# First matrix product of a convolution + MLP kernel issued as 64-row halves, with its weights doubled on both partition halves and partly streamed

## The chip, the cores and the metric

The kernel runs on one core of a Trainium2 chip. A core has a matrix engine (PE, with weight loads listed apart as PEld), a vector engine (DVE), a scalar engine (ACT), a general engine (POOL) and a small engine that here only issues DMAs (SP). The metric is the device time of one execution in microseconds (us). Times in the profile views are in us from the start of the span, unless marked ns.

## The reference

```python
# x (8, 4096, 192), weight (8, 7), w_in (192, 2048), w_out (2048, 192)
w = softmax(weight, axis=-1)                      # 8 heads, 7 taps
x_pad = concatenate([zeros(B, 6, D), x], axis=1)
a[b, s, h*24:(h+1)*24] = sum_k w[h, k] * x_pad[b, s + k, h*24:(h+1)*24]
h = a.reshape(32768, 192) @ w_in
out = (h * sigmoid(1.702 * h)) @ w_out
```

A causal convolution over seven positions with one set of taps per head, then two matrix products with a sigmoid-weighted activation between them. The weights of the products arrive as 64-bit floats.

## The kernel before

**Tiling.** The 32768 tokens are cut into 32 stretches, called bigs, of 1024 tokens: two sequences (n = 0, 1) of 512 tokens, each cut again into two halves of 256 (o = 0, 1). The 2048 hidden features are cut into 16 units of 128. For every big the kernel runs `hidden` (the first product, 16 units) and then `second` (the second product, whose order is written out by hand in `PLAN`, a fast-multiplication scheme of 25 products on sums of blocks of `g` and sums of blocks of `w_out`). Big 0 has its own code (`first_step`, `second_plain`), since the weights are converted from their 64-bit words while it runs.

**The first product.** The operands are split in two parts each, and three products are added up: `upper_high` (weights `wh`, tokens `xh`), `upper_low` (`wl`, `xl`) and `lower` (a ring slot, `xd`). Each of the three is one call of `pass_of`, and there are 48 passes per big. The 192 input features are a block of 128 and a block of 64. A pass is two matmuls over 128 rows (L215, one for each token half o) and two over 64 rows (L221); of the latter, o = 0 lies on partitions 0 to 63 and o = 1 on 64 to 127, and they start together. `phase` turns the order around from pass to pass, so that the 64-row matmuls of two neighbouring passes stand side by side, and the 128-row ones too. All matmuls have 512 columns of tokens and write one PSUM bank each; a unit owns a slot of two banks, and four slots rotate.

**Order in `hidden`.** For unit i the PE order is `upper_high(i)`, `lower(i-2)`, `upper_low(i)`. After `upper_low(i)` the two banks are multiplied by a constant (`scale`, L237, on ACT or DVE as `SCALES` says: "av" is one half on each, "vv" both on DVE). `lower(i)` needs that scale; `gelu` (L241, two ACT instructions) follows it, and `upper_high(i+4)` needs the gelu, as it writes the same slot. `lower(15)` (`end_unit` of the last unit) is issued as `end`, a little into `second`. The call `extra(i)` at the end of unit i puts other work in line: the input of the big after next (`load_x`, SP, at unit 0), the last three convolution taps and their sums (`next_tap`, L500 on ACT at units 0, 2 and 3; `add_taps`, L517, mostly on POOL), three 32x32 transposes of the input on DVE (`transpose_x`, L161, units 7, 8, 9), and the first ten sums of blocks of `g` (`EARLY_G`, L607, units 10 to 15: nine on DVE, one as an accumulating DMA from POOL). The sum of `EARLY_G` listed as number 6 (unit 13) reads what that DMA wrote.

**Weights.** `wh` and `wl` stay in SBUF for all 16 units. The third part is streamed from DRAM through `ring`, six slots of 128 x 256; after `lower` of ring entry q, `load_ring(q + 6)` is issued on SP.

**Queues.** SP issues all input loads, ring loads and output stores in program order; each may wait for a semaphore, and what stands behind it waits too. ACT, DVE and POOL also work strictly in order.

**The start.** In `first_step`, weight piece j (of 8, two units each) goes through `split` (DVE, ACT), `round_w_in` (three DVE instructions, then ACT L437 writes `wh`, POOL L438, ACT `wl`, POOL L440 the ring slot, and SP stores it). This is issued in `extra(i)` for even i, for piece i/2 + 1.

Of the kernel before, what the change touches and what calls it, by code (L numbers as in the profile page):

```python
# [16 lines left out]
def kernel(  # L17
# [27 lines left out]
    NJ2 = TOK // Q + 1  # L45
    n3 = NC * Q
    assert B % 2 == 0 and NC == 3 and D == NC * R and HD == 3 * Q and S % TOK == 0
    assert D == P + R and PAD <= Q
# [65 lines left out]

    turned = [consts.tile([P, 2, n * Q], F32, name=f"xt{i}") for i, n in enumerate((NJ2, NJ))]
    own = consts.tile([P, 6, T], F32)
    flat_own = own.rearrange("p b t -> p (b t)")
    xh, xl, xd = (consts.tile([P, 6, T], F32R, name=f"x{i}") for i in "hld")
    NX1, NX2 = 2 * NJ2 * Q, 2 * NJ * Q

    def xin_of(big):
        flat = flat_room if big == 2 else flat_g(NG - 1)
        return (
            flat[:, 0:NX1].rearrange("p (n j d) -> p n j d", n=2, j=NJ2),
            flat[:, NX1 : NX1 + NX2].rearrange("p (n j d) -> p n j d", n=2, j=NJ),
        )

    def load_x(big, parts=(0, 2, 1)):

        p, c = divmod(big, CHUNKS)  # L130
        one, two = xin_of(big)
        fill = nc.gpsimd if big else vec

        def load(dst, n, t, d, j):
            nc.sync.dma_start(  # L135
                out=dst[:, j:, :],
                in_=x_v[n, p, t + j * Q : t + dst.shape[1] * Q, d : d + Q].rearrange("(j i) d -> i j d", i=Q),
            )

        for a in parts:  # L140
            if a < 2:
                if c == 0:
                    fill.memset(one[:, a, 0, :], 0.0)
                for q in range(4):
                    load(one[q * Q : (q + 1) * Q, a], a, c * TOK - Q, q * Q, int(c == 0))
            else:
                if c == 0:
                    fill.memset(two[0:R, :, 0, :], 0.0)
                for n in range(2):
                    for q in range(4):  # L150
                        o, v = divmod(q, 2)
                        load(
                            two[q * Q : (q + 1) * Q, n], n, c * TOK + o * T - Q, P + v * Q, int(c == 0 and o == 0)
                        )

    def transpose_x(big, a):
        xin = xin_of(big)
        src, dst = (xin[0][:, a], turned[0][:, a]) if a < 2 else (xin[1], turned[1])
        if a == 2:
            src, dst = src.rearrange("p n j d -> p (n j) d"), dst.rearrange("p n t -> p (n t)")  # L160
        vec.transpose(dst.rearrange("p (j t) -> p j t", t=Q), src)  # L161

    def conv_src(a, k):
        at = slice(Q - PAD + k, Q - PAD + k + (TOK if a < 2 else T))
        return turned[0][:, a, at].rearrange("p (o t) -> p o t", o=2) if a < 2 else turned[1][:, :, at]

    def tap_of(a, k):
        return cw[:, a // 2, k : k + 1]

    def own_of(a):  # L170
        return own[:, 2 * a : 2 * a + 2, :]

    def conv(a, k, times=vec.tensor_scalar_mul):
        src, dst, tap = conv_src(a, k), own_of(a), tap_of(a, k)
        if k == 0:
            times(dst, src, tap)
        else:
            vec.scalar_tensor_tensor(  # L178
                out=dst, in0=src, scalar=tap, in1=dst, op0=ALU.mult, op1=ALU.add
            )  # L180
# [18 lines left out]
    wd_dram = dram.tile([N_W, P, 2, 2 * P], F32)  # L199

    def load_ring(q):
        if q < NF * N_BIG:
            r = q % NF
            nc.sync.dma_start(
                out=wide(ring[:, q % RING]).rearrange("p k f -> p (k f)"), in_=wd_dram[r // 2, :, r % 2, :]
            )

    phase = [0]

    def pass_of(slot, w, t, first=False, last=False):  # L210
        phase[0] += 1
        for step in range(2):
            if (step + phase[0]) % 2:
                for o in range(2):
                    nc.tensor.matmul(  # L215
                        slot[o], w[:, 0, :], t[:, o : o + 3 : 2, :],
                        start=first and step == 0, stop=last and step == 1, skip_group_check=True,
                    )
            else:
                for o in range(2):  # L220
                    nc.tensor.matmul(  # L221
                        slot[o], w[halves[o], 1, :], t[halves[o], 4:6, :],
                        start=first and step == 0, stop=last and step == 1, skip_group_check=True,
                    )
# [4 lines left out]
    def upper_low(slot, r):  # L229
        pass_of(slot, wl[:, r], xl)  # L230

    def lower(slot, q):
        pass_of(slot, ring[:, q % RING], xd, last=True)
# [13 lines left out]
    def end_unit(big, tiles, r):  # L247
        q = big * NF + r
        lower(tiles[r % 4], q)
        gelu(tiles[r % 4], r)  # L250
        if q + RING >= NF:
            load_ring(q + RING)

    def hidden(big, tiles, scales, extra, begun=True):

        for i in range(NF):
            if i or not begun:
                upper_high(tiles[i % 4], i)
            if i > 1:
                end_unit(big, tiles, i - 2)  # L260
            if i or not begun:
                upper_low(tiles[i % 4], i)
            scale(tiles[i % 4], scales[i])
            extra(i)
# [50 lines left out]
    PART = 4 * P  # L315
    PIECE = CW * D
    raw = [flat_g(2)[:, 2 * PART * i : 2 * PART * (i + 1)] for i in range(4)]
    free = flat_g(3)[:, NX1 + NX2 :]
    raw += [free[:, 2 * PART * i : 2 * PART * (i + 1)] for i in range(2)]
    raw += [osbs[:, 0 : 2 * PART], flat_own[:, 0 : 2 * PART]]  # L320
    raw_out = [flat_room[:, 2 * PIECE * i : 2 * PIECE * (i + 1)] for i in range(3)] + [osbs[:, 0 : 2 * PIECE]]
    assert 2 * PART <= 4 * T and NX1 + NX2 + 4 * PART <= 4 * BLK and 6 * PIECE <= 5 * BLK
    words_in = [flat_form[:, 2 * PART * i : 2 * PART * (i + 1)] for i in range(3)]
    words_out = [flat_form[:, 6 * PART + 2 * PIECE * i : 6 * PART + 2 * PIECE * (i + 1)] for i in range(2)]
    assert 6 * PART + 4 * PIECE <= FORMS * NG * HD
    diag = flat_room[:, 4 * PIECE : 4 * PIECE + K * P].rearrange("p (k q) -> p k q", k=K)
    all_sel = osbs[:, 2 * PIECE : 2 * PIECE + 2 * P].rearrange("i (c q) -> i c q", c=2)
    sel = all_sel[0:H]
    ident = osbs[:, 2 * PIECE + 2 * P : 2 * PIECE + 3 * P]
    assert 2 * PIECE + 3 * P <= 4 * TOK  # L330
# [10 lines left out]
    load_x(0, (0, 2))  # L341

    w_in_v = moe_w_in.bitcast(U32)
    w_out_v = moe_w_out.bitcast(U32).rearrange("(c p) d -> p c d", p=P)

    def load_w_in(j):
        dst = raw[j].bitcast(U32).rearrange("p (r k f) -> p r k f", r=2, k=2)
        cols = slice(4 * P * j, 4 * P * (j + 1))
        for on, k, rows in ((slice(0, P), 0, 0), (halves[0], 1, P), (halves[1], 1, P)):
            n = on.stop - on.start  # L350
            nc.sync.dma_start(
                out=dst[on, :, k, :], in_=w_in_v[rows : rows + n, cols].rearrange("q (r f) -> q r f", r=2)
# [9 lines left out]
    load_x(0, (1,))  # L362
# [4 lines left out]
    for c in range(2):  # L367
        part = sel[:, c, :].rearrange("i (h q) -> i h q", h=2)
        for sign in (1, -1):
# [5 lines left out]
                base=P * c if sign == 1 else group - 1 - P * c,  # L375
                pattern=[[0 if c else sign * R, 2], [sign, R]],
# [14 lines left out]
    def in_part(j):  # L391
        return raw[j], words_in[j % 3]
# [35 lines left out]
    def round_w_in(j):  # L428
# [3 lines left out]
        w, rest = m.bitcast(F32), e.bitcast(F32)  # L432
        rounded(piece, [(lambda a: a, w)])
        flat = [t[:, 2 * j : 2 * j + 2].rearrange("p r k f -> p (r k f)") for t in (wh, wl)]
        at = 2 * j % RING
        low = ring[:, at : at + 2].rearrange("p r k f -> p (r k f)")
        act.mul(flat[0], w, DOWN)  # L437
        nc.gpsimd.tensor_sub(rest, w, wide(flat[0]))  # L438
        act.mul(flat[1], rest, C)
        nc.gpsimd.tensor_sub(low, wide(flat[1]), wide(flat[0]))  # L440
        nc.sync.dma_start(out=wd_dram[j].rearrange("p r f -> p (r f)"), in_=wide(low))
# [17 lines left out]
    pw = pairs[0][0][:, 0 : 2 * P].rearrange("p (c k) -> p c k", c=2)  # L459
# [6 lines left out]
    for c in range(2):  # L466
# [4 lines left out]
    share = consts.tile([P, 2, 1], F32)  # L471
    vec.tensor_scalar_add(share, pw[:, :, K : K + 1], 1e-9)
    vec.reciprocal(share, share)
    cw = consts.tile([P, 2, K], F32)
    vec.tensor_tensor(out=cw, in0=pw[:, :, 0:K], in1=share.to_broadcast([P, 2, K]), op=ALU.mult)
# [217 lines left out]
    def first_conv(a):  # L693

        for k in range(K):
            nc.tensor.matmul(
                pairs[1][a], diag[:, k, :], conv_src(a, k), start=(k == 0), stop=(k == K - 1), skip_group_check=True
            )

    def first_src(a):  # L700
        return (own_of(2) if a == 2 else pairs[1][a].rearrange("p (o t) -> p o t", o=2)), 2 * a, 2 * a + 2

    def first_step(tiles):

        for k in range(K):
            act.mul(diag[:, k, :], ident, cw[:, 0, k : k + 1])
        transpose_x(0, 0)
        first_conv(0)
# [154 lines left out]
```

## Time and profile before

| | us |
|---|---|
| median of three runs | 2587.68 (2587.56 to 2588.02) |
| profiled execution, its own time | 2591.83 |
| its span, first to last instruction | 2589.9 |
| mean granted PE clock | 0.991 |

A row of a group or timeline view reads: engine, line of the kernel, operation, tiles written <- tiles read, shapes, count; then busy time and mean ns of one (groups), or start and length in us at the head of the row (timelines; neighbouring instructions of one kind are merged with a count), and in brackets the idle time before, and what ended it. Lengths of neighbouring instructions of one engine overlap by some tens of ns, so start-to-start distances are used for sums. In a row of stretches, each engine has its busy time and its instruction count.

### The profile page before, as it was taken

How to read it: one execution, taken by the hardware profiler on the slowest of the kernel's cores; microseconds unless marked ns; L12 is line 12 of the kernel's file. 1: busy time of each engine (PE TensorE's matmuls, PEld its weight loads, DVE VectorE, ACT ScalarE, POOL GpSimd, SP SyncE). 2: the span in 40 equal slices, each digit the busy share in tenths (PEclk: the TensorE clock that was granted, in tenths of full speed). 3: DMA queues.
4: the chain of work that ended last, by engine and by line, in shares of the span. 5: the costliest groups of instructions: out<-in, count | busy, mean ns of one | idle time of the engine just before them, and what ended most of it. 6: DMA issues, size and time to landing. Idle time of an engine off the chain costs nothing.

```text
span 2589.9 us, 63267 instructions
## 1 busy us (share of the span) xinstructions
PE 2526.6 (98%) x25920; PEld 1395.9 (54%) x25920; DVE 1861.0 (72%) x2631; ACT 1569.4 (61%) x3034; POOL 745.9 (29%) x738
## 2 busy tenths in 40 slices
PE   7969999999999999999999999999999999999999
PEld 3335555555555555555555555555555555555555
DVE  5747877667877767776767776777776777776676
ACT  5536665666665666665666656666656666656643
POOL 2203222333232333132333222332223332223300
PEclk9979999999999999999999999999999999999999
DMA  5436654666554666555666545666545666545543
GB/s 148 88 75 128 121 108 102 119 121 131 117 105 101 125 122 130 112 105 103 127 123 125 114 103 105 132 122 120 114 100 113 125 128 121 109 100 118 109 85 73
DMA packets 463809, 293.30 MB, mean 113 GB/s; under 512 B 336672, under 2 KB 408992, under 8 KB 463520
## 3 DMA queue, kind: packets, MB, share of 16 engines
q0 software_dynamic: 63216, 162.49, 35.1%
q1 hardware_dynamic: 398656, 126.37, 20.9%
q8 instruction: 205, 3.36, 0.5%
q14 instruction: 84, 0.69, 0.1%
q10 hardware_dynamic: 1648, 0.39, 0.1%
HBM read 99.42 MB, written 27.26 MB: 49 GB/s over the span
## 4 chain that ended last, share of the span: by engine, by line
PE 89%; ACT 5%; DVE 4%; DMA 1%; issue 1%; POOL 0%; SPq 0%; DVEq 0%; POOLq 0%
PE slot L544 37%; PE slot L215 33%; PE slot L221 19%; ACT g L241 3%; ACT xh L183 2%; DVE g L607 1%; DVE own L178 1%; DMA w_form<-w_form 1%; ACT room L655 0%; POOL w_form L306 0%; SPq L135 0%; DVE w_form L411 0%; DVE w_form L408 0%; DVE w_form L419 0%; ACT wh L437 0%
## 5 line engine op out<-in xcount | busy, mean ns | idle before, releaser
L544 PE MATMUL slot<-g,w_form 128*32 128x256 f32 x8928 | 906.6, 380 | 0.0
L241 ACT ACTIVATE g<-slot 128x512 f32<-128x512 f32 x1024 | 554.8, 595 | 500.6 <-PE slot L215 271.2
L237 DVE TENSOR_SCALAR slot<-slot 128x512 f32<-128x512 f32 x737 | 491.3, 694 | 483.0 <-PE slot L215 242.3
L544 PEld LDWEIGHTS slot<-g,w_form 128*32 128x32 f32 x8928 | 475.4, 110 | 144.2 <-issue 11.3
L607 DVE TENSOR_TENSOR g<-g 128x1024 f32<-128x1024 f32 x403 | 484.9, 1216 | 69.0 <-ACT g L241 67.6
L544 PE MATMUL slot<-g,w_out_s 128*32 128x256 f32 (+1 forms) x6336 | 512.2, 394 | 18.7 <-DVE g L607 14.8
L655 ACT COPY room<-slot 32x256 f32<-32x256 f32 x651 | 237.7, 365 | 301.9 <-PE slot L544 295.4
L544 PEld LDWEIGHTS slot<-g,w_out_s 128*32 128x32 f32 x6336 | 254.2, 110 | 228.2 <-issue 33.4
L215 PE MATMUL slot<-xh,wh 128*128 128x512 f32 x1024 | 352.2, 425 | 11.2 <-ACT wh L437 7.5
L215 PE MATMUL slot<-xl,wl 128*128 128x512 f32 x1024 | 356.6, 429 | 0.0
L215 PE MATMUL slot<-xd,ring 128*128 128x512 f32 x1024 | 351.8, 425 | 0.4 <-ACT slot L237 0.4
L500 ACT ACTIVATE g<-xt,cw 128x512 f32<-128x512 f32 x406 | 286.4, 719 | 62.7 <-POOL own L517 57.5
L612 POOL DMA_DIRECT2D g<-g x124 | 120.1, 968 | 557.3 <-PE slot L544 536.0
L221 PE MATMUL slot<-xd,ring 64*128 64x512 f32 x1024 | 234.7, 454 | 24.2 <-ACT slot L237 12.3
L215 PEld LDWEIGHTS slot<-xh,wh 128*128 128x128 f32 x1024 | 172.9, 189 | 134.1 <-issue 95.6
L215 PEld LDWEIGHTS slot<-xl,wl 128*128 128x128 f32 x1024 | 170.9, 189 | 129.0 <-issue 106.2
L215 PEld LDWEIGHTS slot<-xd,ring 128*128 128x128 f32 x1024 | 173.4, 189 | 115.2 <-issue 90.9
L221 PE MATMUL slot<-xh,wh 64*128 64x512 f32 x1024 | 234.1, 454 | 0.0
L517 POOL TENSOR_TENSOR own<-own,g 128x512 f32<-128x512 f32 x174 | 232.1, 1354 | 4.6
L221 PE MATMUL slot<-xl,wl 64*128 64x512 f32 x1024 | 227.7, 441 | 0.0
L544 PE MATMUL slot<-osbs,w_form 128*32 128x256 f32 x2232 | 225.3, 379 | 0.0
L237 ACT ACTIVATE slot<-slot 128x512 f32<-128x512 f32 x287 | 167.6, 584 | 71.0 <-PE slot L215 55.1
(109 smaller groups left out, 2476.7 us busy)
## 6 DMA issues: line engine op xcount, KB each, us to landing
ring<-wd_dram SPq DMA_DIRECT2D x496, 128.0 KB, 2.1
g<-g POOLq DMA_DIRECT2D x124, 512.0 KB, 7.8
out_dram<-osbs SPq DMA_DIRECT2D x186, 128.0 KB, 2.5
g<-osbs POOLq DMA_DIRECT2D x31, 512.0 KB, 4.9
g<-room POOLq DMA_DIRECT2D x31, 512.0 KB, 4.9
g<-room POOLq DMA_DIRECT2D x58, 256.0 KB, 6.4
g<-g POOLq DMA_DIRECT2D x58, 256.0 KB, 7.1
g<-in_x_dram SPq DMA_DIRECT2D x216, 68.0 KB, 2.6
```

The costliest lines, as they stand in the source:

```text
L178: vec.scalar_tensor_tensor(out=dst, in0=src, scalar=tap, in1=dst, op0=ALU.mult, op1=ALU.add)
L183: act.mul(xh[:, b0:b1, :], src, DOWN)
L215: nc.tensor.matmul(slot[o], w[:, 0, :], t[:, o : o + 3 : 2, :], start=first and step == 0, stop=last and step == 1, skip_group_check=True,)
L221: nc.tensor.matmul(slot[o], w[halves[o], 1, :], t[halves[o], 4:6, :], start=first and step == 0, stop=last and step == 1, skip_group_check ...
L237: (act.mul if engines[o] == "a" else vec.tensor_scalar_mul)(slot[o], slot[o], UP)
L241: act.activation(g[:, r // NG, :, o, r % NG, :], slot[o].rearrange("p (n t) -> p n t", n=2), AF.Gelu_apprx_sigmoid,)
L500: act.mul(home, conv_src(c, k), tap_of(c, k))
L517: eng.tensor_add(dst, dst, home)
L544: nc.tensor.matmul(dst, w, t, start=first, stop=last, skip_group_check=True)
L607: (vec.tensor_add if op == "+" else vec.tensor_sub)(v(dst), v(a), v(b))
L612: nc.gpsimd.dma_start(out=spot(dst), in_=spot(a), accum_op=ALU.add)
L655: act.copy(to, d)
```

## The change

The input features become three blocks of 64 (`NC` = 3), and every block has the two token halves o on the two partition halves. A pass is three pairs of 64-row matmuls (`KS`), with no 128-row matmul left. The weights are therefore needed twice, on partitions 0 to 63 and again on 64 to 127. `wh` stays whole in SBUF (three blocks in place of two), `wl` stays for even units only; `wl` of odd units and the whole third part are streamed through `ring`, now seven slots of 128 x 384: 24 entries per big, each loaded by two DMAs of 64 x 384. The input is loaded by 24 DMAs of 32 x 9 x 32 in place of 16 (eight of 32 x 17 x 32 and eight of 32 x 9 x 32), three at each of units 0 to 7; the transposes stand at units 9 to 11. `SCALES` moves three half scales per big from DVE to ACT. In the start, a weight piece is rounded on 64-row halves (384 words in place of 512), copied by four DMAs to both halves (`both`), and split from there (`split_w_in`), with three DMAs to DRAM; for big 0 the convolution of blocks 1 and 2 runs on PE and of block 0 on DVE.

```diff
-    wh, wl = (consts.tile([P, NF, 2, P], F32R, name=f"w{i}") for i in "hl")
-    RING = 6
-    ring = consts.tile([P, RING, 2, P], F32R)
+    wh = consts.tile([P, NF, NC, P], F32R)
+    wl = consts.tile([P, NF // 2, NC, P], F32R)
+    RING = 7
+    ring = consts.tile([P, RING, NC, P], F32R)
...
+    def place(what, r):
+        return 3 * (r // 2) + (0 if what == "l" else 1 + r % 2)
...
     def load_ring(q):
-        if q < NF * N_BIG:
...
+        if q < STREAM * N_BIG:
+            for o in range(2):
+                nc.sync.dma_start(
+                    out=wide(in_ring(q))[halves[o]].rearrange("p k f -> p (k f)"), in_=w_dram[q % STREAM]
+                )
...
+    def later(q):
+        if q + RING >= STREAM:
+            load_ring(q + RING)
+
+    KS = (1, 2, 0)
+
     def pass_of(slot, w, t, first=False, last=False):
...
+        for k in KS:
+            for o in range(2):
+                nc.tensor.matmul(
+                    slot[o], w[halves[o], k, :], t[halves[o], 2 * k : 2 * k + 2, :],
+                    start=first and k == KS[0], stop=last and k == KS[-1], skip_group_check=True,
+                )
...
+    def upper_low(slot, r, big):
+        if r % 2:
+            q = STREAM * big + place("l", r)
+            pass_of(slot, in_ring(q), xl)
+            later(q)
+        else:
+            pass_of(slot, wl[:, r // 2], xl)
+
+    def lower(slot, r, big):
+        q = STREAM * big + place("d", r)
+        pass_of(slot, in_ring(q), xd, last=True)
+        later(q)
...
+        both = both_in[j % 2]
+        for h in range(2):
+            for o in range(2):
+                nc.sync.dma_start(out=both[halves[o], h * PART : (h + 1) * PART], in_=w[halves[h], :])
+
+    def split_w_in(j):
+        both = both_in[j % 2]
+        act.mul(wh[:, 2 * j : 2 * j + 2].rearrange("p r k f -> p (r k f)"), both, DOWN)
+        nc.gpsimd.tensor_sub(both, both, wide(wh[:, 2 * j : 2 * j + 2].rearrange("p r k f -> p (r k f)")))
+        lows = [t.rearrange("p k f -> p (k f)") for t in (wl[:, j], in_ring(place("l", 2 * j + 1)))]
+        for h in range(2):
+            act.mul(lows[h], both[:, h * PART : (h + 1) * PART], C)
+        for h in range(2):
+            r = 2 * j + h
+            to = in_ring(place("d", r)).rearrange("p k f -> p (k f)")
+            nc.gpsimd.tensor_sub(to, wide(lows[h]), wide(wh[:, r].rearrange("p k f -> p (k f)")))
+        for q in range(3 * j, 3 * j + 3):
+            nc.sync.dma_start(out=w_dram[q], in_=wide(in_ring(q))[0:R].rearrange("p k f -> p (k f)"))
...
         for k in range(K):
+            conv(0, k)
         round_w_in(0)
         split(in_part(1))
+        for c in (1, 0, 2):
+            split_high(*first_src(c))
+            split_low(*first_src(c))
+            split_both(*first_src(c))
+        split_w_in(0)
         load_x(1)
         for i in range(3):
             load_w_out(i)
...
-    SCALES = ["av", "av", "av", "vv"] + ["av", "vv"] * 6
+    SCALES = ["av", "vv", "av", "vv", "vv", "av", "vv"] + ["av"] * 9
...
         def extra(i, big=big):
+            if i < 8 and big + 2 < N_BIG:
+                load_x(big + 2, i)
             if i == 0:
-                if big + 2 < N_BIG:
-                    load_x(big + 2)
                 next_tap()
...
-            if i in (7, 8, 9) and big + 2 < N_BIG:
-                transpose_x(big + 2, i - 7)
+            if i in (9, 10, 11) and big + 2 < N_BIG:
+                transpose_x(big + 2, i - 9)
```

More of the change, by code (lines that the diff above doesn't have):

```diff
@@ L121, in xin_of @@
+    NX = 2 * NJ * XW
+    x_p = x_v.rearrange("h p s (c v e) -> h p v s c e", c=NC, e=Q)
     def xin_of(big):
         flat = flat_room if big == 2 else flat_g(NG - 1)
-        return (
-            flat[:, 0:NX1].rearrange("p (n j d) -> p n j d", n=2, j=NJ2),
-            flat[:, NX1 : NX1 + NX2].rearrange("p (n j d) -> p n j d", n=2, j=NJ),
-        )
[L128 to L154, printed above, removed]
@@ L208 @@
-    phase = [0]
-    def pass_of(slot, w, t, first=False, last=False):
[L211 to L224, printed above, removed]
+    STREAM = 3 * N_W
```

184 lines of the change are left out of this document (83 added, 101 removed).

## The prediction, made before the changed kernel ran

> **What bounds the kernel now.** The page comes first: busy shares and the chain that ended last.
>
> ```profile
> span 2589.9 us, 63267 instructions
> PE 2526.6 (98%) x25920; PEld 1395.9 (54%) x25920; DVE 1861.0 (72%) x2631; ACT 1569.4 (61%) x3034; POOL 745.9 (29%) x738
> PE 89%; ACT 5%; DVE 4%; DMA 1%; issue 1%; POOL 0%; SPq 0%; DVEq 0%; POOLq 0%
> ```
>
> PE is busy throughout and is the chain. A share over the span hides stages, so next come stretches: a first product, a second product, and the first 18 us of a first product.
>
> ```profile
> 1098.40:1141.00 42.60, 42.60 (x197) 22.91 (x196) 27.55 (x38) 22.67 (x41) 12.62 (x10) 1.00 0.43 95
> 1141.00:1176.40 35.40, 34.91 (x629) 20.42 (x628) 29.43 (x43) 26.48 (x54) 11.53 (x16) 1.00 0.74 136
> ...
> 1100.60:1119.00 18.40, 18.40 (x83) 9.91 (x81) 7.16 (x11) 11.26 (x20) 11.74 (x9) 1.00 0.55 111
> ```
>
> In the first product PE has no gap, while DVE works 27.55 of 42.6 us, ACT 22.67, POOL 12.62. Only the first product is changed. Its PE timeline, and below it the weight loads:
>
> ```profile
> 1179.12 0.50 PE L221 MATMUL slot<-xh,wh 64*128 64x512 f32 x2
> 1179.46 0.40 PE L221 MATMUL slot<-xl,wl 64*128 64x512 f32 x2
> 1179.79 0.73 PE L215 MATMUL slot<-xl,wl 128*128 128x512 f32 x2
> 1180.36 0.63 PE L215 MATMUL slot<-xh,wh 128*128 128x512 f32 x2
> 1180.92 0.51 PE L221 MATMUL slot<-xh,wh 64*128 64x512 f32 x2
> ```
>
> ```profile
> 1179.12 0.19 PEld L221 LDWEIGHTS slot<-xh,wh 64*128 64x128 f32 x2 [0.36 <-issue]
> 1179.23 0.19 PEld L221 LDWEIGHTS slot<-xl,wl 64*128 64x128 f32 x2
> ```
>
> From one 64-row group to the next is 1.80 us for two passes: six steps of 512 columns (two pairs, four 128-row matmuls). A step inside a mode is 0.235 (row 1180.36: 0.63 less one matmul of 0.40). Six would be 1.41; the other 0.39 lies at the two switches, where the new mode's weights load only when its first matmul is due (row 1179.12), and the old one is waited out.
>
> **PE in the changed kernel.** A pass is three pairs, with no switch. The trace never has three pairs in a row. Bounds of a pair: 0.23, the step inside a mode, and 0.34, what the first pair takes with its load exposed (1179.12 to 1179.46). I take 0.235: the second pair's loads (row 1179.23) start under the first pair's matmuls and take 0.19, done before 1179.46. A pass is then 0.705 instead of 0.90, a unit 2.115, and 48 passes give 9.4 us per big.
>
> The Trainium skill, "TensorE: Matmul & The Clock Gate", Part 3, says weight loads overlap running matmuls only when the row group differs. The row at 1179.23 disagrees: both loads run under matmuls of their own row groups. By the rule every pair would cost 0.34; that is rival three.
>
> **What is late next: SP.** Zero is the scale of unit 0 (1178.53).
>
> ```profile
> 1178.53 0.58 ACT L237 ACTIVATE slot<-slot 128x512 f32<-128x512 f32 x1 [1.34 <-PE slot L215]
> 1179.14 0.72 ACT L500 ACTIVATE g<-xt,cw 128x512 f32<-128x512 f32 x1
> ...
> 1188.12 0.72 ACT L500 ACTIVATE g<-xt,cw 128x512 f32<-128x512 f32 x1 [2.01 <-POOL own L517]
> 1188.75 1.06 ACT L241 ACTIVATE g<-slot 128x512 f32<-128x512 f32 x2
> ```
>
> ```profile
> 1176.19 4.21 SPq L541 DMA_DIRECT2D out_dram<-osbs  x6
> 1180.50 8.18 SPq L135 DMA_DIRECT2D g<-in_x_dram  x16
> ```
>
> ```profile
> L135 SPq DMA_DIRECT2D g<-in_x_dram x496: 311/455/1842, 0.8 to 2361.9; - x166
> ...
> DMA to landing us min/median/max: 1.8/2.3/4.2
> ```
>
> ```profile
> L204 SPq DMA_DIRECT2D ring<-wd_dram x496: 319/320/1194, 73.1 to 2536.5; - x166
> ...
> DMA to landing us min/median/max: 1.9/2.1/5.6
> ```
>
> Three half scales per big move from DVE to ACT, 0.58 each (row 1178.53). That is 1.8 us for ACT, which works 22.67 us where the new stage has some 33: idle time hides it, and without that each would hold up a gelu by 0.5. Convolution taps, splits and sums keep their sizes and stay hidden as they are; the three memsets of the first big of a sequence become one, outside the chain.
>
> SP begins the input loads at 1.97, behind six stores. Each issue holds it 0.455 us, 0.50 with the gap to the next (16 in 8.18). In the changed kernel the last input part, at unit 7, has 21 input issues and 20 ring issues (ten entries) ahead of it: 21 x 0.50 = 10.5. A ring issue of 64 rows isn't in the trace; bounds 0.37 (the 128-row issue, 0.32, with gap) and 0.50 (as an input load); I take 0.42, nearer the ring's own row: 8.4. The part is issued at 1.97 + 10.5 + 8.4 = 20.9 and lands 2.3 later: 23.2 (22.2 to 24.8). PE unhindered reaches the transposes at 1.4 + 8 x 2.115 + 0.6 = 18.9, so DVE stands in the first of them, and unit 10's scale and the sums queue behind it. The ring keeps up: an entry is loaded four to five units, over 8 us, ahead; SP lags by some 5, a landing takes 2.1.
>
> **Then DVE.** It has three transposes and nine sums in units 9 to 15.
>
> ```profile
> 1203.06 0.77 DVE L161 STREAM_TRANSPOSE xt<-g 128x576 f32<-128x576 f32 x1
> 1204.80 0.70 DVE L237 TENSOR_SCALAR slot<-slot 128x512 f32<-128x512 f32 x1 [0.97 <-ACT g L241]
> 1205.41 1.22 DVE L607 TENSOR_TENSOR g<-g 128x1024 f32<-128x1024 f32 x1
> 1206.66 1.23 DVE L607 TENSOR_TENSOR osbs<-g 128x1024 f32<-128x1024 f32 x1
> 1207.80 1.29 DVE L237 TENSOR_SCALAR slot<-slot 128x512 f32<-128x512 f32 x2
> ```
>
> ```profile
> 1213.44 0.39 PE L221 MATMUL slot<-xd,ring 64*128 64x512 f32 x2
> ...
> 1217.91 0.62 PE L215 MATMUL slot<-xd,ring 128*128 128x512 f32 x2
> ...
> 1220.76 0.51 PE L221 MATMUL slot<-xd,ring 64*128 64x512 f32 x2
> ```
>
> ```profile
> 1208.44 0.88 POOL L612 DMA_DIRECT2D g<-osbs  x1 [16.51 <-DVE osbs L607]
> ```
>
> ```profile
> g<-osbs POOLq DMA_DIRECT2D x31, 512.0 KB, 4.9
> ```
>
> Start to start: scale 0.61, sum 1.14, transpose 0.68 (0.77 less the overlap of 0.09 that the others show). From 23.2: first transpose 0.68, units 10 and 11 each 0.61 + 0.68 + 2 x 1.14 = 3.57, so unit 12's scale starts at 31.0, and with its 0.70 and an assumed 0.05 for the signal, `lower(12)` starts at 31.75. Before, it starts at 1213.44, that is 34.9. From there DVE needs 2 x 1.75 for units 12 and 13 and 2.89 for unit 14: scale 15 ends at 38.1; PE needs five passes (3.5) and the stretch from `lower(14)` to `lower(15)` (2.85, one switch less): 38.0. The sum behind the accumulating DMA is due at 33.4. That DMA is issued 0.55 after its source's sum ends (1207.89 to 1208.44), here 27.5, and takes 4.9: it lands at 33.0, in time. So `lower(15)` starts at 38.1 instead of 42.2 (1220.76): 4.1 gained, and 0.3 in the three passes outside this stretch: 4.4 per big (2.8 to 5.4 by the landing). The second product hangs on `lower(15)` as before.
>
> Where loads come early, something else waits: the tap of unit 3 stands until 9.6 for POOL's sums (row 1188.12), which PE doesn't hasten. The gelus of unit 2 behind it then end at 11.3 (1188.12 to 1188.75 and 1.06 more). `upper_high(6)` needs their slot and is due at 9.5: unit 5's scale at 1.41 + 4 x 2.115, less the 0.4 by which the next pass starts ahead of it. So 1.9 is lost there. And counted from unit 9's scale, DVE ends scale 12 at 10.0 (2.1 + 2 x 3.57 + 0.75), due at 8.75 (3 x 2.115, four passes, less 0.4): 1.25. That caps the gain at 9.4 - 1.9 - 1.3 = 6.2.
>
> The gain moves one for one with the landing. 29 bigs load input: 29 x 4.4 = 128 (81 to 157). Big 30 has the tap wait alone (9.4 - 1.9), big 31 nothing: 17.
>
> **The start is longer.**
>
> ```profile
> L437 ACT ACTIVATE wh<-w_form x8: 629/629/630, 20.6 to 75.0; 128x512 fp32r<-128x512 f32 x8
> ```
>
> ```profile
> L438 POOL TENSOR_TENSOR w_form<-w_form,wh x8: 1261/1284/1288, 21.4 to 75.7; 128x512 f32<-128x512 f32 x8
> ```
>
> ```profile
> 24.76 0.52 SPq L441 DMA_DIRECT2D wd_dram<-ring  x1
> 25.38 10.05 SPq L135 DMA_DIRECT2D g<-in_x_dram  x16
> 35.47 1.78 SPq L356 DMA_DIRECT2D room<-in_moe_w_out_dram  x3
> ```
>
> ```profile
> L178 DVE SCALAR_TENSOR_TENSOR own<-xt,cw,own 128x512 f32<-128x512 f32 x42 | 31.2, 750 | 1.3
> ```
>
> ```profile
> L419 DVE SCALAR_TENSOR_TENSOR w_out_s<-w_form x8: 551/555/558, 85.5 to 96.3; 128x384 f32<-128x384 f32 x8
> ```
>
> Before, the last `wh` is written at 75.0. After: the 24 input loads hold SP until 12.8 (24 x 0.50) and the weights behind them land near 18. On DVE then follow one `split` (0.8), seven taps (7 x 0.79 with gaps: 5.5) and the rounding (three at 384 words, 0.555 each less overlap: 1.5), so piece 0 is rounded at some 25.5 and copied (four issues and a landing) by 30. Its POOL work grows from 2 x 1.28 to 1.9 + 2 x 1.0 (by width) and ends at 35.5. The stores wait for that, and behind them on SP stand 24 loads (12.0), three `w_out` loads (1.8) and only then the copies of piece 1: landed at 55. Each further piece is a chain: scale 0.7, rounding 1.5, copies 1.5 and landing 2.2, ACT 0.85, POOL 1.9, ACT 0.5, a pass with its drain 1.0 = 10.2. Six: the last `wh` at 117, 42 later (25 if a piece takes 9 and loads issue faster, 60 if landings take the ring's 5.6).
>
> **Sum.** 2591.8 - 128 - 17 + 42 = 2489 in the profiled execution, which is 4.1 above the median: 2485 on the runs. With the bounds: 2438 to 2550.
>
> **Rivals.**
> One, PE's full gain: no queue bites, as now PE alone is the bound: 31 x 9.4 = 291, less 42: 2338. Against it stand the tap's fixed wait and SP's 44 issues. Chance 0.08.
> Two, slower: landings. SP's DMAs take eight semaphores in turn, so an issue waits for the landing of the eighth before it; the issue of 1842 ns beside a median of 455 looks like that. The last part then lands at 1.97 + 49 x landing / 8. The kernel is slower from 0.86 gained per big downward, a landing at 26.7, so from 4.0 us per DMA. For it: the DMA share of 0.55 in those 18 us, to which 2 MB of ring come. Against: median landing 2.3. At 4.5, 1.9 lost per big: 2668. Chance 0.17.
> Three, weight loads stay exposed: a pass 1.02, 48 x 0.12 = 5.8 lost per big: 2588 + 180 + 42 = 2810. Against: row 1179.23. Chance 0.05.
> Four, the 0.39 isn't the switch, and a pass stays 0.90: 2588 + 42 = 2630. Against: steps inside a mode. Chance 0.04.
>
> **How the numbers follow.** The forecast has 0.66. No change means within 0.2%, about what a measurement of this kernel can tell. Faster: 0.66 + 0.08 + the mildest of rival two, 0.76; same 0.02; slower 0.22. The range 2395 to 2600 holds the forecast with an error of its costs and the mild half of rival two.
>
> **What would show it.** Pairs 0.235 apart, no 128-row matmul in the first product. SP without idle time from unit 0 to past unit 7, the last input part landed near 23. DVE idle before the first transpose, ended by a DMA; PE idle before `lower(12)`, ended by DVE L237's line. The last `wh` near 117. Wrong if the transposes find their data, if PE waits for a ring load, or if the pairs are further apart.

## The result, and the profile after

The changed kernel took 2664.28 us (median of 4 runs, 2662.94 to 2669.02), the kernel before beside it 2587.85: a ratio of 1.0298, 95% interval 1.0280 to 1.0315. It is slower by 3%, where 2485 (2395 to 2600) was predicted. The first page lines of after:

```profile
span 2662.8 us, 72405 instructions
PE 2345.8 (88%) x28994; PEld 1561.1 (59%) x28994; DVE 1799.4 (68%) x2536; ACT 1601.5 (60%) x3142; POOL 754.4 (28%) x742
```

PE works 181 us less than before and now stands idle for 317 (before 63). So the work on PE did get shorter; the time went into waits. The waits of PE and of DVE in after (engine, line <- releaser: us in total, times, longest):

```profile
PE slot L209 <- DVE slot L232: 104.6, 86, 11.9
PE slot L209 <- DMA ring<-w_dram: 69.4, 111, 2.7
PE slot L209 <- ACT wh L429: 53.7, 8, 22.5
PE slot L209 <- ACT g L236: 38.1, 29, 1.3
```

```profile
DVE xt L143 <- DMA g<-in_x_dram: 213.4, 30, 8.5
```

Four waits: for VectorE's scale (L232), for ring entries, for `wh` at the start, and for the gelu at `upper_high(6)`. Behind the first stands the second fence: VectorE's transposes wait for the input, 7.1 us in each big. Such waits may lie one behind the other, so they aren't added up; the experiments below tell them apart.

Three stretches give the sum. `hidden(2)` starts at 290.2 (before 238.5): the start is 51.7 longer, of which big 1 is a part. From there to the start of `hidden(30)` lie 28 periods, in the first row of each of the two fences below (start and end, us, then busy time of PE, PEld, DVE, ACT and POOL with instructions, granted clock, DMA share, GB/s), before's first:

```profile
238.46:2427.95 2189.49, 2175.99 (x22852) 1213.60 (x22849) 1598.01 (x2240) 1376.47 (x2660) 670.31 (x653) 1.00 0.59 116
```

```profile
290.20:2516.70 2226.50, 2020.65 (x25540) 1352.99 (x25537) 1546.44 (x2156) 1401.55 (x2744) 668.21 (x647) 0.98 0.70 148
...
2516.70:2588.00 71.30, 68.68 (x918) 47.10 (x914) 53.26 (x74) 37.99 (x80) 16.91 (x15) 1.00 0.52 124
```

A period is 2226.5 / 28 = 79.52 against 78.20: 1.3 lost per big, not 4.4 gained. Big 30, which loads no input, takes 71.3: 6.9 gained. So the same PE program does gain where SP has no input to issue.

Now one big in the middle. Its scale of unit 0, the zero of the prediction, starts at 1165.21:

```profile
1165.21 0.58 ACT L232 ACTIVATE slot<-slot 128x512 f32<-128x512 f32 x1 [1.16 <-PE slot L209]
```

SP's queue in this big (start, us, operation, times), and its ring issues in the whole run (shortest, median and longest in ns); the `EVENT_SEMAPHORE` rows are SP's waits ahead of these issues:

```profile
1163.04 3.75 SPq L539 DMA_DIRECT2D out_dram<-osbs  x6
1166.89 1.48 SPq L137 DMA_DIRECT2D g<-in_x_dram  x3
1168.47 1.09 SPq L196 DMA_DIRECT2D ring<-w_dram  x2
...
1188.37 2.38 SPq L196 DMA_DIRECT2D ring<-w_dram  x4
1190.79 1.57 SPq L137 DMA_DIRECT2D g<-in_x_dram  x3
1192.46 20.70 SPq L196 DMA_DIRECT2D ring<-w_dram  x28
```

```profile
L196 SPq EVENT_SEMAPHORE  x1488: 17/17/17, 134.3 to 2614.0; - x186
L196 SPq DMA_DIRECT2D ring<-w_dram x1488: 444/546/2584, 134.3 to 2614.1; - x186
...
DMA to landing us min/median/max: 2.2/2.4/5.6
```

From 1166.89 to 1213.16 SP issues one transfer after the other: its longest gap there is 0.35 us, and the last 28 issues come 0.74 apart on average. A ring issue of 64 rows holds it 0.546 us, 0.59 with the gap (2.38 for four). The last input part is issued at 1190.79, 25.6 after zero. What follows on VectorE and TensorE:

```profile
1185.46 0.70 DVE L232 TENSOR_SCALAR slot<-slot 128x512 f32<-128x512 f32 x1 [1.73 <-PE slot L209]
1193.04 0.78 DVE L143 STREAM_TRANSPOSE xt<-g 128x576 f32<-128x576 f32 x1 [6.88 <-DMA g<-in_x_dram]
...
1200.88 0.70 DVE L232 TENSOR_SCALAR slot<-slot 128x512 f32<-128x512 f32 x1
```

```profile
1190.61 0.49 PE L209 MATMUL slot<-xl,ring 64*128 64x512 f32 x1 [0.96 <-DMA ring<-w_dram]
...
1201.63 0.96 PE L209 MATMUL slot<-xd,ring 64*128 64x512 f32 x5 [1.18 <-DVE slot L232]
1202.21 1.08 PE L209 MATMUL slot<-xl,wl 64*128 64x512 f32 x6
1202.90 1.08 PE L209 MATMUL slot<-xh,wh 64*128 64x512 f32 x6
...
1208.14 1.07 PE L209 MATMUL slot<-xd,ring 64*128 64x512 f32 x6
```

VectorE stands idle for 6.88 until the input lands; `lower(12)` starts at 1201.63, 36.4 after zero, and `lower(15)` at 1208.14, 42.9 after zero (before 42.2). Passes follow each other by 0.69 (1202.21 to 1202.90). The start, at last:

```profile
L429 ACT ACTIVATE wh<-w_form x8: 842/842/843, 30.1 to 128.3; 128x768 fp32r<-128x768 f32 x8
```

The last `wh` is written at 128.3 (before 75.0, predicted 117).

### The profile page after: what moved, and what is told of

Its sections match the earlier page's. It is cut to its first block, busy times and chain, and to the rows that moved or that the text cites. A ratio compares the mean times of both kernels' runs of the same rounds, so it can differ in the third digit from the quotient of the medians.

```text
span 2662.8 us, 72405 instructions
## 1 busy us (share of the span) xinstructions
PE 2345.8 (88%) x28994; PEld 1561.1 (59%) x28994; DVE 1799.4 (68%) x2536; ACT 1601.5 (60%) x3142; POOL 754.4 (28%) x742
## 5 line engine op out<-in xcount | busy, mean ns | idle before, releaser
L232 DVE TENSOR_SCALAR slot<-slot 128x512 f32<-128x512 f32 x644 | 435.1, 694 | 438.1 <-PE slot L209 404.9
L209 PE MATMUL slot<-xd,ring 64*128 64x512 f32 x3072 | 573.1, 411 | 129.2 <-DVE slot L232 104.6
L209 PE MATMUL slot<-xh,wh 64*128 64x512 f32 x3072 | 541.5, 408 | 91.8 <-ACT wh L429 53.7
L605 DVE TENSOR_TENSOR g<-g 128x1024 f32<-128x1024 f32 x403 | 484.6, 1215 | 38.1 <-ACT g L236 29.0
L209 PEld LDWEIGHTS slot<-xd,ring 64*128 64x128 f32 x3072 | 355.9, 191 | 252.7 <-DVE slot L232 156.3
L209 PEld LDWEIGHTS slot<-xh,wh 64*128 64x128 f32 x3072 | 359.1, 193 | 186.1 <-ACT g L236 60.1
L209 PE MATMUL slot<-xl,ring 64*128 64x512 f32 x1536 | 280.0, 409 | 60.7 <-DMA ring<-w_dram 59.7
L232 ACT ACTIVATE slot<-slot 128x512 f32<-128x512 f32 x380 | 228.6, 602 | 123.6 <-PE slot L209 123.4
L209 PE MATMUL slot<-xl,wl 64*128 64x512 f32 x1536 | 262.9, 402 | 1.5 <-ACT wl L433 1.5
L209 PEld LDWEIGHTS slot<-xl,ring 64*128 64x128 f32 x1536 | 174.1, 189 | 123.7 <-DMA ring<-w_dram 98.7
L143 DVE STREAM_TRANSPOSE xt<-g 128x576 f32<-128x576 f32 x93 | 71.2, 767 | 213.4 <-DMA g<-in_x_dram 213.4
```

The source lines that it names most:

```text
L143: vec.transpose(xt[:, c, :, :].rearrange("p n (j t) -> p (n j) t", t=Q), xin_of(big).rearrange("p n j d -> p (n j) d")[:, :, c * Q : (c + ...
L209: nc.tensor.matmul(slot[o], w[halves[o], k, :], t[halves[o], 2 * k : 2 * k + 2, :], start=first and k == KS[0], stop=last and k == KS[-1], ...
L232: (act.mul if engines[o] == "a" else vec.tensor_scalar_mul)(slot[o], slot[o], UP)
L605: (vec.tensor_add if op == "+" else vec.tensor_sub)(v(dst), v(a), v(b))
```

## The experiments

The question is which of three holds the steady stages: the number of SP's issues, the bytes and landings of the doubled transfers, or PE itself; and then what the start is made of. Ratios are to the kernel before, run on the same chip.

**One transfer for a ring entry.** The DRAM copy of the streamed weights keeps both halves, and an entry is loaded by one transfer of 128 rows. The same bytes reach the ring.

```diff
-    w_dram = dram.tile([STREAM, R, NC * P], F32)
+    w_dram = dram.tile([STREAM, P, NC * P], F32)
...
-            for o in range(2):
-                nc.sync.dma_start(
-                    out=wide(in_ring(q))[halves[o]].rearrange("p k f -> p (k f)"), in_=w_dram[q % STREAM]
-                )
+            nc.sync.dma_start(out=wide(in_ring(q)).rearrange("p k f -> p (k f)"), in_=w_dram[q % STREAM])
...
-            nc.sync.dma_start(out=w_dram[q], in_=wide(in_ring(q))[0:R].rearrange("p k f -> p (k f)"))
+            nc.sync.dma_start(out=w_dram[q], in_=wide(in_ring(q)).rearrange("p k f -> p (k f)"))
```

> The changed kernel with each ring entry loaded by one DMA of 128 x 384 instead of two of 64 x 384 (DRAM holds both halves; the same bytes are loaded). Theory 'SP issue': 10 ring issues instead of 20 stand ahead of the last input part. At 0.38 us each (estimate: between the 0.32 of the 128 x 256 load before and the 0.55 of the 64 x 384 load after) it lands near 19.5 us after the scale of unit 0 instead of 27.6, so the wait of DVE for input data falls from 213 us to under 30, the ring waits of PE from 69 us to under 10, and the time to 2460 (2440 to 2500). Rival 'transfer': the DMA engines or the landings limit, not the issue; the bytes are the same, the transposes still wait near 200 us, time 2655 to 2670.

Measured: 2449.51 us, ratio 0.9459 (0.9445 to 0.9473). Its ring issues on SP, and its waits:

```profile
L195 SPq DMA_DIRECT2D ring<-w_dram x744: 319/376/2049, 134.0 to 2401.2; - x186
...
DMA to landing us min/median/max: 2.1/2.6/6.7
```

```profile
1170.33 2.43 SPq L137 DMA_DIRECT2D g<-in_x_dram  x3
```

```profile
PE slot L206 <- DVE slot L229: 57.7, 47, 11.9
PE slot L206 <- ACT wh L426: 53.0, 8, 22.1
PE slot L206 <- ACT g L233: 38.0, 29, 1.3
```

```profile
DVE xt L143 <- DMA g<-in_x_dram: 33.7, 25, 8.1
```

The landing is no shorter (2.6), and yet 215 us are gone with 744 issues fewer. An issue of 128 rows holds SP 0.376, less than one of 64. In the big of the row at 1170.33 zero is 1152.59, so the last input part is issued 17.7 after zero, not 25.6; VectorE waits 33.7 for the input, not 213.4 (a little more than the 30 expected), and PE for no ring entry. Issues, not bytes or landings, made the loss. The steady stretch against after's:

```profile
284.20:2305.10 2020.90, 1928.59 (x25540) 1323.68 (x25536) 1547.86 (x2156) 1396.94 (x2744) 668.22 (x647) 1.00 0.77 163
```

72.17 per big, 6.0 less than before the change and 7.3 less than after. PE's idle time accounts for 113.5 of the 205.6 between them (205.9 against 92.3); for the rest its matmuls are recorded longer in after. Some 38 us of that, at most, is the halved clock of the last section, half of the 75 us that it lasted in this stretch; what remains isn't broken down.

**The kernel before, with its own ring loads cut in two.** Nothing else changes.

```diff
-            nc.sync.dma_start(
-                out=wide(ring[:, q % RING]).rearrange("p k f -> p (k f)"), in_=wd_dram[r // 2, :, r % 2, :]
-            )
+            for o in range(2):
+                nc.sync.dma_start(
+                    out=wide(ring[:, q % RING])[halves[o]].rearrange("p k f -> p (k f)"),
+                    in_=wd_dram[r // 2, halves[o], r % 2, :],
+                )
```

> The kernel before, with each ring load cut into two DMAs of 64 x 256 (same bytes). Theory 'SP issue': a 64-row issue holds SP about 0.45 to 0.55 us as in the changed kernel, so an entry costs over 1 us instead of 0.37, but 16 entries and 16 input loads fit into the 43 us of a first product, and time stays within 0.3% of before (2580 to 2596). Rival 'small DMAs land late': PE waits for ring data, 2600 or more. If a 64-row issue here takes 0.32 us, it is the 1536-byte rows that made it dear, not the 64 rows.

Measured: 2588.93 us, ratio 0.9999 (0.9989 to 1.0008).

```profile
L205 SPq DMA_DIRECT2D ring<-wd_dram x992: 444/546/1785, 73.5 to 2534.1; - x199
```

The issue costs 0.546 here too, with rows of 1024 bytes in place of 1536: for this load the 64 rows set it, not the bytes. And in this kernel, with 32 such issues per big, SP has room for it. The price alone isn't the loss; it is the price times 48 in a stage that has just become shorter.

**No input loads.** The changed kernel leaves out the input loads of bigs 3 to 31; it computes on stale data, and serves for its time alone.

```diff
-            if i < 8 and big + 2 < N_BIG:
-                load_x(big + 2, i)
```

> The changed kernel without the input loads of bigs 3 to 31 (their outputs come from stale data; all compute instructions stay). Theory 'SP issue': SP has the ring alone, DVE never waits for input, PE rarely for the ring; what remains per big is the tap wait of 1.9 us at unit 6 and some 1.3 us of DVE queue at unit 12, so a big takes about 72 us instead of 79.5 and the time is 2450 (2425 to 2490). Rival 'ring alone is too slow': 24 entries of 1.28 us keep SP busy 31 us of 34, PE still waits for ring data, 2550 or more.

Measured: 2446.86 us (a single execution, so no interval).

```profile
PE slot L209 <- DVE slot L232: 53.4, 40, 11.9
PE slot L209 <- ACT g L236: 38.1, 29, 1.3
```

The ring is still loaded by 64 rows, and PE waits for none of it. SP is the bound by the sum of both streams: halve the issues of the one or take away the other, and the time is 2447 to 2450. What is left in both are the two waits that the prediction named as the cap: the tap's and VectorE's queue.

**The transposes two units later**, the ring left at 64 rows.

```diff
-            if i in (9, 10, 11) and big + 2 < N_BIG:
-                transpose_x(big + 2, i - 9)
+            if i in (11, 12, 13) and big + 2 < N_BIG:
+                transpose_x(big + 2, i - 11)
```

> The changed kernel, its ring still loaded by two transfers of 64 rows, with the three transposes of the input moved from units 9, 10 and 11 to units 11, 12 and 13 of the first product. Theory, that the late input costs time only through VectorE's queue, where the scales of units 10 to 12 stand behind transposes that wait for data: TensorE's wait for VectorE's scale falls from 104.6 us to under 40, and the time is 2620 (2600 to 2640), the ring's own waits staying. Rival, that SP's stream, which issues input and ring entries in one order, sets the stage's end whatever TensorE waits for in between: what is gained before lower(12) is waited for at the ring, whose wait (69.4 us) rises above 100, and the time is 2650 to 2670.

Measured: 2621.31 us, ratio 1.0135 (1.0114 to 1.0156).

```profile
PE slot L209 <- DMA ring<-w_dram: 92.0, 135, 3.0
...
PE slot L209 <- DVE slot L232: 14.4, 7, 11.9
```

VectorE's queue is worth 43 us by itself. The wait for its scale is all but gone, and the ring's wait rose by 23 of the 90. The period is still 78.0 (from 290.5 to 2475.1), some 5.8 above the 72.2 of one transfer. Both runs have the same wait for the gelu (38.1 and 38.0), so what holds the stage there is the ring, with the slower matmuls that go with its waits. The two waits are two faces of SP's one stream.

**The start.** First only the loads that stand ahead of the second piece's copies are moved:

```diff
         split_w_in(0)
-        load_x(1)
-        for i in range(3):
-            load_w_out(i)
...
+            if i in (1, 3, 5, 7):
+                load_x(1, i - 1)
+                load_x(1, i)
+            if i in (9, 11, 12):
+                load_w_out((9, 11, 12).index(i))
```

> The changed kernel with the input loads of big 1 and the w_out loads taken from ahead of weight piece 1's copies on SP and put into units 1 to 12 of big 0. Theory 'queue in the start': piece 1's copies are issued some 14 us earlier, the second wh is written near 46 instead of 59.3, time 2650 (2647 to 2656). Rival 'chain alone': the start is bound by the chain of rounding, copies and splits and nothing moves, 2660 or more.

Measured: 2657.51 us, ratio 1.0263 (1.0248 to 1.0278), 6.8 less than after and just above the range of the theory. TensorE comes to the second piece 18 sooner (42.0, not 60.2), but the later pieces 13 apart, with the input loads now between their copies on SP. Then, beside this, the copies of each piece one step ahead:

```diff
         round_w_in(0)
         split(in_part(1))
+        round_w_in(1)
...
-                round_w_in(j)
                 if j + 1 < N_W:
                     split(in_part(j + 1))
+                    round_w_in(j + 1)
                 split_w_in(j)
```

> The changed kernel, with the loads of the second group's input and of w_out moved from ahead of the second piece's copies into units 1 to 12 of the first stage, and with the join, the rounding and the four copies of each piece of w_in issued one step earlier, so that a piece's copies travel while the piece before it is split. Theory, that the start is a chain of copies: each piece of wh waits for its own copies (2.4 us issued one after the other on SP, then the landing) and for the splits that the piece before holds up; with the copies one step ahead the pieces come some 7 us apart, not 11.5, the last piece of wh is written near 85, not 128.3, the first stage ends about 40 us sooner, and the time is 2620 (2605 to 2640). Rival, that the start is bound elsewhere (by the splits on ScalarE and GpSimd, or by the input's and w_out's loads, which land later too): the pieces stay 10 to 12 apart and the time is 2645 to 2660.

Measured: 2617.03 us, ratio 1.0104 (1.0089 to 1.0119).

```profile
L429 ACT ACTIVATE wh<-w_form x8: 826/827/859, 30.4 to 82.3; 128x768 fp32r<-128x768 f32 x8
```

The pieces come 7.4 apart and the last at 82.3: ScalarE's wait for the copies falls from 38.5 us to 2.1, and TensorE's wait for `wh` from 53.7 to 9.5. So 47 us of the start were waits for copies that had been issued too late.

**The rest of the waits, with one transfer per ring entry.** Three runs. In the first the third tap moves from unit 3 to unit 4:

```diff
                 add_taps("c2 2", "fin 3")
-                next_tap()
             if i == 4:
+                next_tap()
                 add_taps("c2 5", "c2 6")
```

> The changed kernel with each ring entry again loaded by one transfer of 128 rows, and the third tap of the convolution moved from unit 3 to unit 4 of the first product. Theory, that TensorE's idle time before upper_high(6) comes from the gelu that stands behind this tap in ScalarE's queue, while the tap waits for GpSimd's addition: the wait of TensorE for ScalarE's gelu, 38.0 us in 29 waits where one transfer alone was restored, falls under 10, nothing else moves, and the time is 2415 (2405 to 2430). Rival, that the tap only hides another limit (the adding of taps then ends later, and with it the high split of the next group, or VectorE's scale is next at the same place): 2440 to 2455.

Measured: 2448.98 us, ratio 0.9457 (0.9441 to 0.9473), as without it. A miss.

```profile
PE slot L206 <- DVE slot L229: 97.3, 80, 11.9
```

```profile
DVE xt L143 <- DMA g<-in_x_dram: 92.4, 30, 8.0
```

The wait for the gelu is gone from PE's list (38.0), and the wait for VectorE's scale rose by 39.6. The input's landing, which the tap's stop had covered, is next. So sooner loads? Two input parts in each of units 0 to 3, the transposes at units 7 to 9:

```diff
-            if i < 8 and big + 2 < N_BIG:
-                load_x(big + 2, i)
+            if i < 4 and big + 2 < N_BIG:
+                load_x(big + 2, 2 * i)
+                load_x(big + 2, 2 * i + 1)
...
-            if i in (9, 10, 11) and big + 2 < N_BIG:
-                transpose_x(big + 2, i - 9)
+            if i in (7, 8, 9) and big + 2 < N_BIG:
+                transpose_x(big + 2, i - 7)
```

> The changed kernel with each ring entry loaded by one transfer of 128 rows, and the input loads of the group after next issued two parts per unit in units 0 to 3 (one part in each of units 0 to 7 otherwise), their transposes at units 7 to 9 (9 to 11 otherwise). Theory, that TensorE's idle time before lower(12) is VectorE's queue alone, which holds the scale of unit 12 behind three transposes: with the transposes two units sooner the scale comes in time, the wait of TensorE for VectorE's scale falls from 57.7 us to 20 or less, and the time is 2412 (2400 to 2430). Rival, that the early inputs push the ring's entries behind them on SP and the transposes still wait for data: TensorE waits for the ring, and the time is 2445 to 2480.

Measured: 2470.87 us, ratio 0.9539 (0.9524 to 0.9553): slower than one transfer alone by 21.

```profile
PE slot L206 <- DVE slot L229: 42.4, 34, 11.9
...
PE slot L206 <- DMA ring<-w_dram: 15.7, 30, 1.1
```

The scale's wait fell, but six input issues in a row (2.9 us) take longer than a unit (2.04), and the ring is late. The rival held in its time and in the wait for the ring; its transposes still wait, but less (22.0 us, not 33.7). All of this, the tap's and the start's edits of above included:

> The changed kernel with one transfer of 128 rows for each ring entry, the start reordered as in the run that reorders the start alone, the third tap at unit 4, and the input loads and transposes two units sooner. By the theories of the three other runs, whose gains are at different places and so add up (about 35 for the tap, 35 for the transposes, 40 for the start, off 2449.5): 2340 (2320 to 2370). Rival, that the gains take from one another (SP, which issues both the early inputs and the ring, or VectorE between taps and transposes, is the next bound): 2380 to 2430.

Measured: 2432.25 us, ratio 0.9392 (0.9378 to 0.9406), 2 above the rival's range. PE waited 66.7 for the ring. The gains did not add up. The last two runs go by what these showed. One transfer and the start alone:

> The changed kernel with each ring entry loaded by one transfer of 128 rows and the start reordered (loads of input and w_out moved behind the copies, each piece's copies one step ahead), and nothing else. Theory, that the two losses are at different places and add up: 2449.5 less the 47 that reordering the start gave by itself, so 2403 (2393 to 2415), with the steady period at 72 as with the one transfer alone. Rival, that the 2432 of the run with all four edits shows the start's gain being taken back in the stages behind it: 2425 to 2440.

Measured: 2402.48 us, ratio 0.9282 (0.9268 to 0.9296): these two do add up. And beside them the tap at unit 4 with the transposes one unit later:

```diff
-            if i in (9, 10, 11) and big + 2 < N_BIG:
-                transpose_x(big + 2, i - 9)
+            if i in (10, 11, 12) and big + 2 < N_BIG:
+                transpose_x(big + 2, i - 10)
```

> The changed kernel with one transfer of 128 rows for each ring entry, the start reordered, the third tap at unit 4, and the three transposes one unit later (units 10 to 12). Theory, that with the tap's wait gone the input's landing is what holds TensorE, through the scales behind the transposes, so that later transposes, not earlier loads, free it: TensorE's wait for VectorE's scale falls from 97.3 us under 45, the steady period from 72 to 70.7, and the time is 2365 (2350 to 2385). Rival, that the wait moves on once more (to the ring, or to the gelu of unit 12, which writes the block that the transposes read): 2395 to 2410.

Measured: 2380.75 us, ratio 0.9198 (0.9184 to 0.9212): 22 less than without the last two edits, in the range, though the scale's wait fell less than expected, to 69.6. The period is 71.4, where 70.7 was expected. It is the best of these versions, 8.0% below the kernel before.

## Why the prediction was wrong, point by point

**PE's pace was right.** Predicted 0.235 a pair and 0.705 a pass; measured 0.69 a pass and 2.04 a unit. The third rival (exposed weight loads, 0.34 a pair) and the fourth (a pass stays 0.90) fall with it. The rule of the Trainium skill behind rival three, "TensorE: Matmul & The Clock Gate", Part 3, by which weight loads run under matmuls only of another row group, would have put pairs 0.34 apart; the trace disagrees, with 0.23.

**SP as the next bound was right, its price was not.** This is the step that failed: "A ring issue of 64 rows isn't in the trace; bounds 0.37 [...] and 0.50 [...]; I take 0.42, nearer the ring's own row". It is 0.59 with its gap, outside both bounds. From start to start, the twenty ring issues ahead of the last part took 11.9, not 8.4. The 21 input issues took 12.0, not 10.5: 0.57 each, where 0.50 was read from 16 issues in 8.18, which is 0.51 to begin with. The stores were 0.3 sooner. The last part was issued at 25.6 in place of 20.9 and used at 27.8 in place of 23.2.

Both rows chosen as bounds were on the cheap side: the ring's own row has 128 rows, and here fewer rows cost SP more, not less. The trace of before did hold a nearer row. Of the weight loads in its start, three for each piece, two in three have 64 rows, and they take 0.60:

```profile
L351 SPq DMA_DIRECT2D g<-in_moe_w_in_dram x18: 456/601/720, 6.8 to 19.9; - x18
```

With 0.60 for 0.42, the prediction's own sum has the last part landing at 26.8, 0.8 gained per big in place of 4.4, and about 2589 us: no change, and no longer a gain.

**The chain behind it was right.** From the first transpose to `lower(12)` 8.55 were predicted, 8.59 measured (1193.04 to 1201.63); from there to `lower(15)` 6.35 and 6.5. "The gain moves one for one with the landing" holds: the first transpose is 4.6 late, `lower(15)` 4.8 (42.9 for 38.1). The text even had the point from which the kernel is slower, a landing at 26.7, but hung it on rival two.

**"The ring keeps up" was wrong.** SP lags not by 5 us but to the stage's end; PE waits for entries 111 times, one of the signs that the prediction had named against itself. By the run with later transposes this alone holds the stage near 78. The late input, by the prediction's own chain, turns 4.4 gained into 0.4 lost (4.4 less 4.8); the other 0.9 of the 1.3 lost per big isn't in that chain, and the ring's waits, put at nothing, are what the runs show for it. A sum over SP's whole stage makes it plain: stores 3.9, 24 input issues at 0.57 and 48 ring issues at 0.59 are 46 us, more than the 45.1 from the first store to `lower(15)` (1163.04 to 1208.14). With the prediction's prices it was 36.5, against a forecast of 40.4 for the same stretch: already little room.

**Rival two had the sign, by another mechanism.** It asked for landings of 4.0 us or more; the median is 2.0 for the input and 2.4 for the ring. SP was busy issuing, not held by transfers in flight: the wait ahead of each of its 1488 ring issues took 17 ns. And one transfer of 128 rows, with longer landings, was fast.

**The cap came out, in part by luck.** 6.2 per big was predicted once loads come early; one transfer gives 78.20 - 72.17 = 6.0. Both waits are there. At `upper_high(6)`:

```profile
1163.38 1.22 PE L206 MATMUL slot<-xh,wh 64*128 64x512 f32 x5 [1.30 <-ACT g L233]
```

The passes around it start at 1161.23 and 1164.44, 3.21 apart in place of two passes of 0.68: 1.9 lost, as predicted. At `lower(12)`, with a gap of 1.2, 1.5 is lost in the same way (predicted 1.3). But passes of 0.68 instead of 0.705 gain 48 x 0.22 = 10.6 and not 9.4, and some 1.2 more than these two losses is lost again; where isn't traced, though PE waits for the scale 47 times in this run, more than once in a stage. Big 30 gained 6.9 (7.5). Rival one's 9.4 came in no run; 71.4 a period, 6.8, was the most.

**The start was under-sized.** The chain from piece to piece was right, its steps are longer: 11.5 against 10.2, and the second piece at 59.3 against 55. Of the 1.3 that a step is longer, 0.9 is again the price of issues: the four copies of a piece, of 64 rows each, hold SP 2.4 us, where 1.5 was taken. The last `wh` is 53 later, not 42.

In the profiled execution: 2489 predicted; 14 more from the start (51.7 at `hidden(2)`, where 42 less one big's 4.4 was predicted), 28 x 5.7 = 160 from the periods, 1 from the last two bigs: 2664.

The Trainium skill, "DMA: Bandwidth & Descriptors", "Rules for kernel authors", advises against two transfers to disjoint partition halves and for one of 128 partitions, since both halves share the same DMA engines. The advice holds here, 2449.51 against 2664.28; the reason that the runs show is another, SP's time for the issue, as landings were not longer with halves. It spoke against the change, and the prediction didn't weigh it.

## What to carry to other kernels

When a change makes a stage shorter and cuts its transfers in two, add up the issuing queue over the stage as one does for an engine: issues times price against the stage's new length. Where the price isn't in the trace, look through all of it, the start too, for a transfer of the same shape; a row that is near by its name but not by its shape is no bound, and room must be left on its far side. A wait that is removed on a kernel with several queues near their limit often only uncovers the next one, so what edits gain is measured together, and not added up.

## What the hardware showed that was not expected

An issue of fewer rows is dearer for SP: 0.546 us (median) for 64 rows in both kernels that have them, with 1024 and with 1536 bytes a row, against 0.320 and 0.376 for 128 rows. The shortest are 0.444 and 0.319, and the stores of the ring in the start agree, 0.462 for 64 rows (after) and 0.326 for 128 (one transfer). The rows aren't all of it: the start's weight loads in before, with two runs of 1024 bytes to a row, take 0.60 with 64 and with 128 rows. Why is left open.

Short waits in a row also lower TensorE's clock. In after (us, PE busy with matmuls, granted clock, DMA share, GB/s):

```profile
711.50:713.00 1.50, 0.67 (x6) 1.00 0.20 31
713.00:714.50 1.50, 0.93 (x5) 1.00 0.48 92
714.50:716.00 1.50, 0.78 (x3) 0.60 0.51 152
716.00:717.50 1.50, 1.50 (x9) 0.50 0.53 115
...
720.50:722.00 1.50, 1.50 (x12) 0.62 0.50 151
722.00:723.50 1.50, 1.37 (x12) 1.00 0.50 146
```

After PE's waits of 0.7, 0.6 and 1.1 us from 706.7 on, the clock is halved at 714.8, for 6.8 us, though PE was never idle for longer than 1.1. Of 26 such stages (of the 28), 12 had a mean granted clock of 0.93 or 0.96 over 47 us, which is 6.6 or 3.8 us at half, and 14 had 1.00; with one transfer, where a stage has two gaps of 1.3 and 1.2 some 19 apart, all 28 had 1.00. Over longer stretches the same shows: the granted clock changes in steps of 3.41 us, and from 300 us to the last steady stage of after PE was busy for 22 to 61% of the step ahead of each of the 14 falls to 0.50. Of the 615 steps at full clock that no fall followed, none was busy for less than 51%; with one transfer none was below 61%, and no fall came. So a late ring costs more than its waits. The lost clock is 8 x 0.07 x 47 + 4 x 0.04 x 47 = 34 us over those 26, at most 1.3 per big, for part of it falls into waits. The Trainium skill, "TensorE: Matmul & The Clock Gate", Part 1, has the clock halved after an idle window of about 3.4 us; the 0.50 agrees, but here a window that was busy by half was enough.
